# A gated linear-attention chain with two expert layers on one core: domain weights tied to the attention's end, two products moved from GpSimd to VectorE, chunk 1 written ahead of the later gates, zero matmuls between the first chunks

## The chip, the cores and the metric

The program runs on one core of a Trainium2 chip. The metric is the time of the whole program on the device in microseconds (us), lower is better, as the median of several executions.

## The reference, cut to what matters

Three layers follow each other. The first is a recurrent attention over 2 batches, 8 heads, 768 tokens and heads of 40 numbers:

```python
for t in range(S):
    m_new = np.maximum(f_gate[:, :, t] + m, i_gate[:, :, t])
    f_stab = np.exp(f_gate[:, :, t] + m - m_new)
    i_stab = np.exp(i_gate[:, :, t] - m_new)
    C = f_stab * C + i_stab * np.einsum('bhd,bhe->bhde', vt, kt)
    n = f_stab * n + i_stab * kt
    y[:, :, t] = sigmoid(o_gate[:, :, t]) * (C @ qt) / np.maximum(np.abs(n @ qt), 1.0)
```

Its 1536 x 320 result x goes through a layer of 8 experts, of which a noisy gate picks the best two for each token: `out[token] += weight * (relu(x @ w1[e]) @ w2[e])`, with w1[e] of 320 x 1024. What comes out goes through a second layer of 4 experts, all of which see every token, each weighted by a domain weight `p = domain_probs / (sum + 1e-9)`:

```python
for e in range(4):
    out += p[:, e:e + 1] * (np.maximum(x @ w1[e], 0.0) @ w2[e])
```

## The kernel before, in words

The attention works on chunks of 128 tokens: chunks 0 to 5 are batch 0, chunks 6 to 11 batch 1. Within a chunk the recurrence is a masked product; between chunks a state C of 104 x 164 numbers is carried. One chunk consists of small steps, each a function `o_...`: D0 and D1 (L340) build the decay matrix A of four heads each (a matmul `dp`, an exponential on ScalarE, a triangular mask on GpSimd), G (L353) the decay of the carried state (matmul `gp`, exponential `gb`), S (L363) the products of queries and keys (16 matmuls `sp`), M0 and M1 (L373) multiply A by S on VectorE, qg (L378) scales the queries by gb, kw (L384) weights the keys, U (L399) makes the state's update `up`, Cg (L394) decays the state and Cu (L410) adds the update, inter (L420) and AV (L433) accumulate into `hp` what comes from the state and from the chunk, tp (L443) turns the result, x (L449) divides and applies the output gate, xp (L465) turns x again and lg (L475) makes the gate's logits. A number in brackets stands for the chunk in this text: AV(1) is AV of chunk 1.

The gates come in four parts (PARTS, L31): chunk 0, chunk 1, chunks 2 and 3, chunks 4 and 5, with all 12 chunks' rows of both batches in the partitions. `gates` (L255) makes the running maximum and the sums on VectorE, `gates_terms` (L269) turns them into the operands tk and tq of D and G (for the later parts mostly on ScalarE), and `gates_turn` (L292) makes w_t, the key weights, by a transposition and an exponential. The output gate's sigmoid (L299) needs another function table of ScalarE than the exponentials, so a table load stands before and after it; it runs over a whole batch at once, in place in `xs`, into which `og_load` brings the output gates.

The order around the first chunks is written out by hand (L889 to L946). After that the table STEP (L47) says which steps of which chunks stand together: "inter+0" in row 1 of step i is inter(i), "S+1" is S(i+1). PLAN1 and PLAN2 mix these rows (A) with the routing (r, q, f) and the splitting of the first expert weights (w). `done` keeps a step that was already written from being written twice. Beneath this order a scheduler places each engine's instructions by what it estimates to be ready, with the written order as priority; `tc.issue_after(x)` puts what stands inside it behind x. All loads are issued by SyncE's queue in its order. Buffers limit how early a load can go: three each of qt and kv, two of kp.

PSUM has 8 buffers, handed out in turn. Before the first real matmul 24 matmuls of zeros (L889, WARM) run on TensorE. Once the attention of batch 0 is routed, `moe1` runs the first expert layer, with the attention of batch 1 woven in, and `moe2` the second. The domain weights `prob` (L985 to L990) are written after the attention's end in the program's text, with nothing that ties them to it.

Of the kernel before, what the change touches and what calls it, by code (L numbers as in the profile page):

```python
# [45 lines left out]

STEP = [  # L47
    "U+0 D0+2 D1+2 kw+1 M1+0 loadk+2 lg-2 store-2",
    "tp-1 x-1 qg+1 M0+0 inter+0 load+3 Cg+0",
    "G+2",  # L50
    "xp-1 S+1 AV+0 Cu+0",
]


# [11 lines left out]
def body(ctx: ExitStack, tc: tile.TileContext, d, o, dbg=None):  # L66
# [172 lines left out]
    def fi_load(n):  # L239
        nc.sync.dma_start(fi[:, :, n], d["fi"].rearrange("r k (c l) -> r k c l", c=NC)[:, :, n])  # L240
# [51 lines left out]
    def gates_turn(part):  # L292
        n = PARTS[part]
        pt = psum([P, n.stop - n.start, 4, 32], "pt")
        for c in range(n.start, n.stop):
            nc.tensor.transpose(pt[:, c - n.start].rearrange("t q r -> t (q r)"), awr[:, c, :], ident)
            nc.scalar.activation(w_t[:, c].rearrange("t (q p) -> t q p", q=4), pt[:, c - n.start, :, 0:4], AF.Exp)

    def sigmoid(b, after):  # L299
        with tc.issue_after(after):  # L300
            s1 = nc.scalar.preload_act_table_set("sigmoid_and_others")
        with tc.issue_after(s1.ins):
            s2 = nc.scalar.activation(xs[b], xs[b], AF.Sigmoid)
        with tc.issue_after(s2.ins):
            return nc.scalar.preload_act_table_set("natural_log_exp_and_others").ins

    at2_cm = tc.tile_pool(name="at2", bufs=2, side="right")
    at2 = at2_cm.__enter__()
# [31 lines left out]
    def o_decay(i, g):  # L340
        b, c = divmod(i, NC)
        t = st[i]
        if g == 0:
            t["A"] = at2.tile([P, H, P], F32, name="A", bufs=3)
        hs_ = slice(4 * g, 4 * g + 4)
        A = t["A"][:, hs_]
        dp = psum([P, 4, P], "dp")
        r = slice(32 * (2 * b + g), 32 * (2 * b + g) + 32)
        nc.tensor.matmul(dp, tk[r, c], tq[r, c], start=True, stop=True)
        front["act"] = nc.scalar.activation(A, dp, AF.Exp).ins  # L350
        nc.gpsimd.affine_select(A, A, pattern=[[0, 4], [1, P]], compare_op=ALU.is_ge, fill=0.0, base=0, channel_multiplier=-1)

    def o_gb(i):  # L353

        b, c = divmod(i, NC)
        if c > 0:
            gp = psum([104, 4, P], "gp")
            nc.tensor.matmul(gp, over[b], tq[:, c], start=True, stop=True)
            gb = at2.tile([104, 4, P], F32, name="gb", bufs=3)
            nc.scalar.activation(gb, gp, AF.Exp)  # L360
            st[i]["gb"] = gb

    def o_S(i):  # L363
# [9 lines left out]
    def o_M(i, g):  # L373
        t = st[i]
        hs_ = slice(4 * g, 4 * g + 4)
        t["m", g] = front["dve"] = nc.vector.tensor_mul(t["A"][:, hs_], t["sp", g], t["A"][:, hs_]).ins

    def o_qg(i):  # L378
        if i % NC > 0:
            qg = at2.tile([104, 4, P], F32, name="qg")  # L380
            nc.gpsimd.tensor_mul(qg, st[i]["qt"], st[i]["gb"])
            st[i]["qg"] = qg

    def o_kw(i):  # L384
# [5 lines left out]

    def state(k):
        return Cs[k][:, : 4 * 41].rearrange("r (p e) -> r p e", p=4)

    def o_Cg(i):  # L394
        c = i % NC
        if 0 < c < NC - 1:
            nc.gpsimd.tensor_mul(state(1 - c % 2), state(c % 2), st[i]["gb"][:, :, P - 1 : P].to_broadcast([104, 4, 41]))

    def o_U(i):  # L399
        if i % NC < NC - 1:  # L400
# [9 lines left out]
    def o_Cu(i):  # L410
        c = i % NC
        if c < NC - 1:
            up = st[i]["up"]
            cs = state(1 - c % 2)
            if c == 0:
                nc.vector.tensor_copy(cs, up)
            else:
                nc.vector.tensor_add(cs, up, cs)

    def o_inter(i):  # L420
        c = i % NC
# [59 lines left out]
            nc.tensor.matmul(lp, xts[i % 2][:, k, :], wgn[:, k, : 2 * E1], start=(k == 0), stop=(k == 2))  # L481
        nc.scalar.copy(lgs[b][:, c, :], lp)

    OPS = dict(loadk=o_loadk, load=o_load, D0=lambda i: o_decay(i, 0), D1=lambda i: o_decay(i, 1), G=o_gb, S=o_S, M0=lambda i: o_M(i, 0), M1=lambda i: o_M(i, 1), qg=o_qg, kw=o_kw, Cg=o_Cg, U=o_U, Cu=o_Cu, inter=o_inter, AV=o_AV, tp=o_tp, x=o_x, store=o_store, xp=o_xp, lg=o_lg)
    done = set()

    def do(op, i, *a):
        if 0 <= i < NT and (op, i) not in done:
            done.add((op, i))
            OPS[op](i, *a)  # L490

# [394 lines left out]
    def og_load(b):  # L886
        nc.sync.dma_start(xs[b], d["og"][b])

    if WARM:  # L889
        wps = psum([P, 4 * P], "warm")  # L890
        for i in range(WARM):
            nc.tensor.matmul(wps, zero[:, :P], zero, start=(i == 0), stop=(i == WARM - 1))
    do("loadk", 0)
    o_load(0, ("qt",))
    fi_load(slice(2, NC))
    o_load(0, ("kv",))
    og_load(0)
    do("loadk", 1)
    o_load(1)
    nc.sync.dma_start(wgn, d["wgn"])  # L900
    exps = nc.scalar.preload_act_table_set("natural_log_exp_and_others").ins
    with tc.issue_after(last_const):
        last = gates(0)
    with tc.issue_after(last), tc.issue_after(exps):
# [2 lines left out]
    do("S", 0)  # L907
    for op in ("D0", "D1"):
        do(op, 0)
    with tc.issue_after(last):  # L910
        over = [at.tile([P, 104], F32R, name=f"over_{b}") for b in range(B)]
        for b in range(B):
            wide = pro.tile([P, 104], F32, name=f"wide_{b}")
            nc.gpsimd.memset(wide, 0.0)
            for j in range(2):
                nc.vector.tensor_mul(wide[:, 64 * j : 64 * j + D], sums.to_broadcast([P, D]), quarter[:, 2 * b + j : 2 * b + j + 1].to_broadcast([P, D]))
            nc.vector.tensor_copy(over[b], wide)
        last = gates(1)
    with tc.issue_after(last):
        last = gates_terms(1)  # L920
# [1 line left out]
        do(op, 0)  # L922
    gates_turn(1)
    do("U", 0)
    do("inter", 0)
    do("AV", 0)
    do("Cu", 0)
    for op in ("D0", "D1", "G", "S"):
        do(op, 1)
    exps = sigmoid(0, front["act"])  # L930
    done.update((("load", 0), ("load", 1)))
# [3 lines left out]
        last = gates(2)  # L935
    with tc.issue_after(last), tc.issue_after(exps):
        last = gates_terms(2)
    gates_turn(2)
    nc.sync.dma_start(noise, d["noise"])
    og_load(1)  # L940
# [41 lines left out]
        weave(moe1(n), RST, 1, 1)  # L982
    drain(RST)
    drain(A)
    nc.sync.dma_start(prob, d["prob"])  # L985
    nc.vector.tensor_reduce(psm, prob, AX.X, ALU.add)
    nc.vector.tensor_scalar(psm, psm, 1e-9, None, ALU.add)
    nc.vector.reciprocal(psm, psm)
    nc.vector.tensor_mul(prob, prob, psm.unsqueeze(2).to_broadcast([P, NT, E2]))
    nc.sync.dma_start(Pall.rearrange("t p e -> p t e"), prob)  # L990
    if dbg == "x":
        for b in range(B):
            nc.sync.dma_start(o["x"][b].rearrange("p c d -> p c d"), xs[b])
# [93 lines left out]
```

## Time and profile before

| what | us |
|---|---|
| median of 3 runs | 720.25 (720.1 to 725.9) |
| the profiled execution, whole | 719.56 |
| its span, first to last instruction | 717.8 |
| TensorE busy in the span | 690.1 (96%) |
| VectorE busy | 367.1 (51%) |
| ScalarE busy | 258.1 (36%) |
| GpSimd busy | 95.3 (13%) |

The profiled execution is one of the same kernel; 1.8 us of it lie outside the span. Times in the trace count from the span's first instruction. TensorE's clock has two levels: 1.2 and 2.4 GHz. The profile gives the granted share of the higher one, so 0.50 is 1.2 GHz and 1.00 is 2.4 GHz. PE is TensorE, DVE VectorE, ACT ScalarE, POOL GpSimd and SP SyncE; SPq is the queue that issues loads.

### The profile page before, as it was taken

To read this page: it belongs to the slowest core of one execution; us is meant where nothing else is said; L and a number is where in the kernel's file an instruction comes from. 1 tells how busy PE (TensorE), PEld (TensorE's weight loads), DVE (VectorE), ACT (ScalarE), POOL (GpSimd) and SP (SyncE) were. 2 spreads that over 40 slices of the span, in tenths; PEclk is the share of its full clock that TensorE was granted. 3 is DMA by queue.
4 is the path that set the end of the run, shared out by engine and by line. 5 is a ranking of instruction groups with operands and counts; after the bars stand their busy time and mean duration, and the time that the engine had idled before them with its cause. 6 is when DMAs were issued, how large, how long until landed. Compare 5 with 4: busy or idle time off the path is not lost.

```text
span 717.8 us, 11459 instructions
## 1 busy us (share of the span) xinstructions
PE 690.1 (96%) x4528; PEld 625.2 (87%) x4528; DVE 367.1 (51%) x806; ACT 258.1 (36%) x477; POOL 95.3 (13%) x155
## 2 busy tenths in 40 slices
PE   7698879999999999999999999999999999999997
PEld 3476658998999999999989898898998988989987
DVE  7635885798466656657865515413244123332131
ACT  3847532555245434444552304212133022221120
POOL 3423334100522011015105000000000000000000
PEclk8569856999999999999999999999999999999999
DMA  8326554546565444458654003200031001001011
GB/s 268 86 88 205 162 166 134 152 136 221 171 193 154 144 143 138 135 155 253 215 179 129 0 1 86 77 1 0 13 104 47 1 0 36 3 1 37 1 37 40
DMA packets 36434, 73.79 MB, mean 103 GB/s; under 512 B 7576, under 2 KB 14744, under 8 KB 36376
## 3 DMA queue, kind: packets, MB, share of 16 engines
q1 hardware_dynamic: 33752, 64.16, 29.0%
q0 software_dynamic: 2624, 8.85, 4.3%
q8 instruction: 38, 0.62, 0.4%
q14 instruction: 20, 0.16, 0.1%
HBM read 64.07 MB, written 8.92 MB: 102 GB/s over the span
## 4 chain that ended last, share of the span: by engine, by line
PE 82%; DMA 7%; DVE 6%; issue 1%; ACT 1%; SPq 1%; ACTq 0%; DVEq 0%
PE z L207 24%; PE z L221 24%; PE s L207 12%; PE s L221 10%; DMA raw<-w 3%; DMA kv<-kv 2%; PE hp L438 2%; PE hp L431 2%; PE sp L370 2%; PE s L217 1%; DVE w1lo L188 1%; PE lp L481 1%; DMA raw<-v 1%; DMA prob<-prob 1%; PE pa L651 1%
## 5 line engine op out<-in xcount | busy, mean ns | idle before, releaser
L224 ACT ACTIVATE hh<-z 128x512 fp32r<-128x512 f32 x96 | 57.1, 599 | 192.4 <-PE z L207 192.2
L221 PE MATMUL z<-w2hi,hh 128*128 128x320 f32 x384 | 118.6, 309 | 0.0
L221 PE MATMUL z<-w2hi,hl 128*128 128x320 f32 x384 | 118.3, 308 | 0.0
L221 PE MATMUL z<-w2lo,hh 128*128 128x320 f32 x384 | 118.3, 308 | 0.0
L207 PE MATMUL z<-x2h,w1hi 128*128 128x512 f32 x288 | 112.4, 390 | 0.0
L221 PE MATMUL s<-w2hi,hh 128*128 128x320 f32 x448 | 107.4, 312 | 1.3 <-DVE hh L225 0.8
L225 DVE SCALAR_TENSOR_TENSOR hl<-z,hh 128x512 fp32r<-128x512 f32 x96 | 65.8, 690 | 82.5 <-ACT hh L224 82.5
L207 PE MATMUL z<-x2h,w1lo 128*128 128x512 f32 x288 | 96.6, 389 | 0.0
L207 PE MATMUL s<-xh,w1hi 128*128 128x256 f32 (+1 forms) x288 | 85.4, 313 | 0.0
L188 DVE TENSOR_TENSOR w2lo<-raw,w2hi 128x640 fp32r<-128x640 f32 x60 | 49.2, 821 | 65.0 <-ACT w2hi L187 64.9
L221 PEld LDWEIGHTS s<-w2hi,hh 128*128 128x128 f32 x448 | 76.7, 188 | 2.4 <-DVE hh L225 1.3
L207 PE MATMUL z<-x2l,w1hi 128*128 128x512 f32 x192 | 74.8, 390 | 0.0
L188 DVE TENSOR_TENSOR w1lo<-raw,w1hi 128x768 fp32r<-128x768 f32 x60 | 58.1, 969 | 31.5 <-ACT w1hi L187 31.3
L187 ACT CAST w2hi<-raw 128x640 fp32r<-128x640 f32 x60 | 43.5, 728 | 84.2 <-PE s L217 25.1
L221 PEld LDWEIGHTS z<-w2lo,hh 128*128 128x128 f32 x384 | 72.1, 188 | 0.6
L221 PEld LDWEIGHTS z<-w2hi,hh 128*128 128x128 f32 x384 | 72.1, 188 | 0.5
L221 PEld LDWEIGHTS z<-w2hi,hl 128*128 128x128 f32 x384 | 72.1, 188 | 0.0
L207 PE MATMUL s<-xh,w1lo 128*128 128x256 f32 (+1 forms) x288 | 70.6, 309 | 0.0
L221 PE MATMUL s<-w2lo,hh 128*128 128x320 f32 x224 | 69.2, 309 | 0.0
L187 ACT CAST w1hi<-raw 128x768 fp32r<-128x768 f32 x60 | 50.2, 836 | 50.2 <-PE s L207 29.2
L207 PEld LDWEIGHTS z<-x2h,w1lo 128*128 128x128 f32 x288 | 54.1, 188 | 11.3
L207 PEld LDWEIGHTS z<-x2h,w1hi 128*128 128x128 f32 x288 | 54.1, 188 | 10.8
(206 smaller groups left out, 1004.4 us busy)
## 6 DMA issues: line engine op xcount, KB each, us to landing
raw<-w SPq DMA_DIRECT2D x44, 384.0 KB
raw<-w SPq DMA_DIRECT2D x44, 320.0 KB
raw<-v SPq DMA_DIRECT2D x16, 384.0 KB
raw<-v SPq DMA_DIRECT2D x16, 320.0 KB
kv<-kv SPq DMA_DIRECT2D x12, 324.0 KB
Yd<-ys SPq DMA_DIRECT2D x8, 320.0 KB
kp<-kT SPq DMA_DIRECT2D x12, 208.0 KB
qt<-qT SPq DMA_DIRECT2D x12, 208.0 KB
```

The lines of the kernel that those rows point to most:

```text
L187: nc.scalar.copy(hi, raw)
L188: nc.vector.tensor_sub(lo, raw, hi.bitcast(F32))
L207: nc.tensor.matmul(out_ps, l, r, start=(i == 0), stop=(i == len(seq) - 1))
L217: nc.tensor.matmul(yp, both[f], r[:, k], start=(f == 0 and i == 0), stop=(f == NF - 1 and i == 1))
L221: nc.tensor.matmul(yp, l, r, start=(f == 0 and i == 0), stop=(f == NF - 1 and i == 2))
L224: nc.scalar.activation(hh, src, AF.Relu)
L225: nc.vector.scalar_tensor_tensor(hl, src, 0.0, hh.bitcast(F32), ALU.max, ALU.subtract)
L370: nc.tensor.matmul(sp[g][:, j, :], t["kp"][r, j, :], t["qt"][r, j, :], start=True, stop=True)
L431: nc.tensor.matmul(hp[64 * j : 64 * j + m, p, :], Cs[c % 2][r, 41 * p : 41 * p + m], t["qg"][r, p, :], start=(p == 0), stop=False)
L438: nc.tensor.matmul(hp[64 * j : 64 * j + 41, p, :], t["kv"][:, 4 * j + p, D:], t["A"][:, 4 * j + p, :], start=False, stop=(p == 3))
L481: nc.tensor.matmul(lp, xts[i % 2][:, k, :], wgn[:, k, : 2 * E1], start=(k == 0), stop=(k == 2))
L651: nc.tensor.transpose(pk[k][:, c], xe[:r, s, k * P : (k + 1) * P], ident[:r, :r])
```

## The change

1. The domain weights' load and their four VectorE operations stand inside `behind()`, so behind the last load, exponential and mask product that the attention issued.
2. qg goes from GpSimd to VectorE (10 products of 104 x 512). Cg, the decay of the state on GpSimd, goes; Cu does both in one operation per head pair, so four operations of 104 x 41 on VectorE in place of one addition of 104 x 164.
3. The gate operands `over` are made on GpSimd and not on VectorE.
4. D, G and S of chunk 1 are written ahead of inter(0) and AV(0), and kw, M, qg, U, Cu, inter and AV of chunk 1 ahead of the third part of the gates. In STEP Cg goes, and xp stands at the end of its row.
5. The first table load ahead of each sigmoid is no longer written out, and each exponential of D and G is tied behind the load that brings the exponentials' table back.
6. Matmuls of zeros (`fill`) stand at four further places: 8, 6, 4 and 12.
7. The load order: kv(0) ahead of the later gates, and chunk 1's loads ahead of the output gates.

```diff
-            s1 = nc.scalar.preload_act_table_set("sigmoid_and_others")
-        with tc.issue_after(s1.ins):
             s2 = nc.scalar.activation(xs[b], xs[b], AF.Sigmoid)
         with tc.issue_after(s2.ins):
-            return nc.scalar.preload_act_table_set("natural_log_exp_and_others").ins
+            front["table"] = nc.scalar.preload_act_table_set("natural_log_exp_and_others").ins
+        return front["table"]
...
-        front["act"] = nc.scalar.activation(A, dp, AF.Exp).ins
+        with tc.issue_after(front["table"]):
+            front["act"] = nc.scalar.activation(A, dp, AF.Exp).ins
...
-            nc.gpsimd.tensor_mul(qg, st[i]["qt"], st[i]["gb"])
+            nc.vector.tensor_mul(qg, st[i]["qt"], st[i]["gb"])
...
-    def o_Cg(i):
-        c = i % NC
-        if 0 < c < NC - 1:
-            nc.gpsimd.tensor_mul(state(1 - c % 2), state(c % 2), st[i]["gb"][:, :, P - 1 : P].to_broadcast([104, 4, 41]))
...
-                nc.vector.tensor_add(cs, up, cs)
+                for p in range(4):
+                    nc.vector.scalar_tensor_tensor(cs[:, p], state(c % 2)[:, p], st[i]["gb"][:, p, P - 1 : P], up[:, p], ALU.mult, ALU.add)
...
+    def fill(n):
+
         wps = psum([P, 4 * P], "warm")
-        for i in range(WARM):
-            nc.tensor.matmul(wps, zero[:, :P], zero, start=(i == 0), stop=(i == WARM - 1))
+        for i in range(n):
+            nc.tensor.matmul(wps, zero[:, :P], zero, start=(i == 0), stop=(i == n - 1))
...
     do("loadk", 0)
     o_load(0, ("qt",))
+    o_load(0, ("kv",))
     fi_load(slice(2, NC))
-    o_load(0, ("kv",))
-    og_load(0)
     do("loadk", 1)
     o_load(1)
+    og_load(0)
...
+    fill(8)
...
     do("U", 0)
+    do("Cu", 0)
+    fill(6)
+    for op in ("D0", "D1", "G", "S"):
+        do(op, 1)
+    fill(4)
     do("inter", 0)
     do("AV", 0)
-    do("Cu", 0)
-    for op in ("D0", "D1", "G", "S"):
+    for op in ("kw", "M0", "M1", "qg", "U", "Cu"):
         do(op, 1)
     exps = sigmoid(0, front["act"])
...
         last = gates_terms(2)
+    do("inter", 1)
+    do("AV", 1)
+    fill(12)
     gates_turn(2)
...
-    nc.sync.dma_start(prob, d["prob"])
...
+    with behind():
+        nc.sync.dma_start(prob, d["prob"])
...
```

What this does to the engines' orders is seen at three places. The first is TensorE around AV(0): before, hp_315 is chunk 0's accumulator (L426 opens it, L438 is AV), dp_329 and dp_333 are D of chunk 1, gp_337 is G(1) and sp_341 and sp_342 are S(1).

```order
L426 LDWEIGHTS zero
L426 MATMUL hp_315<-zero 105x512
L438 MATMUL hp_315<-A,kv 41x128 x8
L349 MATMUL dp_329<-tq,tk 128x512
L349 MATMUL dp_333<-tq,tk 128x512
L358 MATMUL gp_337<-tq,over_270 104x512
L370 MATMUL sp_341<-qt,kp 128x128
```

The same place with the change, where dp_333 and dp_337 are D of chunk 1, gp_341 is G(1), sp_345 and sp_346 are S(1), warm_325 is the last of six matmuls of zeros; AV(0) follows behind S(1) and four more matmuls of zeros:

```order
L890 LDWEIGHTS zero
L890 MATMUL warm_325<-zero 128x512
L348 MATMUL dp_333<-tq,tk 128x512
L348 MATMUL dp_337<-tq,tk 128x512
L358 MATMUL gp_341<-tq,over_279 104x512
L371 MATMUL sp_345<-qt,kp 128x128
L371 MATMUL sp_346<-qt,kp 128x128
```

D, G and S of chunk 1 moved from behind AV(0) to ahead of it.

The second place is TensorE around inter(1): before, it is hp_478 (L431) and stands behind D of chunk 3 (dp_423), the turn of the last gates (pt_453, L296) and tp(0) (tp_462).

```order
L349 MATMUL dp_419<-tq,tk 128x512
L349 MATMUL dp_423<-tq,tk 128x512
L296 MATMUL pt_453<-ident,awr 128x128
L446 MATMUL tp_462<-ident,hs 128x105 x4
L431 MATMUL hp_478<-qg,C_186 64x128
L431 MATMUL hp_478<-qg,C_186 41x128
```

With the change it is hp_420; AV(1) (L435) stands right behind it, then 12 matmuls of zeros, and only then the turn of the third part of the gates, D of chunks 2 and 3 and tp(0):

```order
L428 MATMUL hp_420<-qg,C_186 64x128
L428 MATMUL hp_420<-qg,C_186 41x128
L435 MATMUL hp_420<-A,kv 41x128 x8
L890 LDWEIGHTS zero
L890 MATMUL warm_439<-zero 128x512
```

inter(1) and AV(1) moved from behind tp(0) to ahead of everything that the third part of the gates feeds.

The third place is VectorE behind the sums of the third part of the gates (L263), before and with the change in one piece. psm and prob are the domain weights, A<-sp are M0 and M1 of chunk 1, asr and awr the rest of the gates.

```order
 L263 SCALAR_TENSOR_TENSOR LF<-reset,lf 128x256
-L986 TENSOR_REDUCE psm<-prob 128x12
+L382 TENSOR_TENSOR qg<-qt,gb 104x512
+L377 TENSOR_TENSOR A<-sp_345,A 128x512
+L377 TENSOR_TENSOR A<-sp_346,A 128x512
 L265 TENSOR_TENSOR asr<-fi,LF 128x256
-L987 TENSOR_SCALAR psm<-psm 128x12
 L266 TENSOR_TENSOR awr<-asr,LF 128x256
-L988 RECIPROCAL psm<-psm 128x12
-L376 TENSOR_TENSOR A<-sp_341,A 128x512
-L376 TENSOR_TENSOR A<-sp_342,A 128x512
-L989 TENSOR_TENSOR prob<-prob,psm 128x48
```

The domain weights left this place; qg(1) came in, and chunk 1's M stands ahead of asr and awr.

## Rows read from the trace of the kernel before

**Rows 1.** Stretches of the span; us, busy per engine (instructions), granted PE clock, DMA share, GB/s

```profile
0.00:11.00 11.00, 8.34 (x43) 3.90 (x43) 7.43 (x31) 2.06 (x4) 5.65 (x57) 1.00 0.77 258
11.00:48.00 37.00, 29.39 (x189) 20.41 (x191) 20.70 (x51) 24.55 (x59) 12.19 (x17) 0.50 0.43 120
48.00:79.50 31.50, 26.98 (x339) 20.73 (x333) 20.22 (x60) 20.45 (x40) 11.18 (x14) 0.99 0.61 186
79.50:86.00 6.50, 6.50 (x49) 5.33 (x47) 4.35 (x17) 3.64 (x9) 1.22 (x2) 0.50 0.37 136
86.00:93.00 7.00, 4.85 (x62) 3.71 (x63) 6.46 (x17) 3.26 (x8) 3.57 (x4) 0.99 0.50 163
93.00:120.30 27.30, 24.00 (x183) 19.54 (x180) 20.13 (x75) 8.50 (x19) 11.46 (x12) 0.50 0.53 157
120.30:717.80 597.50, 590.05 (x3678) 551.55 (x3674) 287.83 (x558) 195.66 (x340) 50.04 (x51) 1.00 0.30 91
```

**Rows 2.** Timeline of PE, 0 to 60 us; start, us, engine, line, what, [idle before, releaser]

```profile
1.39 6.71 PE L892 MATMUL warm<-zero 128*128 128x512 bf16 x24 [1.39 <-POOL zero L84]
...
11.68 0.47 PE L296 MATMUL pt<-ident,awr 128*128 128x128 f32 x1 [1.94 <-DVE awr L266]
...
31.09 0.91 PE L446 MATMUL tp<-ident,hs 105*128 105x105 f32 x4
31.93 1.96 PE L431 MATMUL hp<-qg,C 40*64 40x128 f32 x16
...
43.48 0.94 PE L446 MATMUL tp<-ident,hs 105*128 105x105 f32 x4
```

**Rows 3.** Timeline of ACT, 0 to 60 us

```profile
18.00 1.09 ACT L350 ACTIVATE A<-dp 128x512 f32<-128x512 f32 x2
...
20.89 1.80 ACT L303 ACTIVATE x<-x 128x1920 f32<-128x1920 f32 x1
22.71 1.28 ACT L305 ACT_TABLE_LOAD   x1
24.00 0.41 ACT L272 CAST LFh<-LF 128x256 fp32r<-128x256 f32 x1
...
24.62 0.60 ACT L277 ACTIVATE LF<-LF,mix,kind 128x256 f32<-128x256 f32 x1
...
25.77 2.44 ACT L289 ACTIVATE tq<-LF,head 128x128 fp32r<-128x128 f32 x8
```

**Rows 4.** Timeline of DVE, 0 to 45 us

```profile
13.21 0.33 DVE L416 COPY C<-up 104x164 f32<-104x164 f32 x1 [1.59 <-PE up L407]
...
22.84 0.20 DVE L986 TENSOR_REDUCE psm<-prob 128x12 f32<-128x48 f32 x1 [4.81 <-DMA prob<-prob]
...
25.25 0.48 DVE L278 SCALAR_TENSOR_TENSOR LF<-LFh,mix,LF 128x256 f32<-128x256 f32 x1
...
26.22 0.49 DVE L388 TENSOR_TENSOR kw<-kv,w_t 128x320 f32<-128x320 f32 x1
```

**Rows 5.** SP's queue, 0 to 60 us

```profile
12.45 0.33 SPq L887 DMA_DIRECT2D x<-og  x1
```

**Rows 6.** Timeline of ACT again, around the second sigmoid

```profile
54.10 1.28 ACT L360 ACT_TABLE_LOAD   x1 [0.19 <-PE gp L358]
...
59.42 0.57 ACT L440 COPY hs<-hp 105x512 f32<-105x512 f32 x1
```

**Rows 7.** Timeline of DVE, 57 to 126 us

```profile
69.06 1.56 DVE L388 TENSOR_TENSOR kw<-kv,w_t 128x320 f32<-128x320 f32 x1
```

**Rows 8.** Timeline of POOL, 0 to 130 us

```profile
68.92 1.35 POOL L381 TENSOR_TENSOR qg<-qt,gb 104x512 f32<-104x512 f32 x1 [1.40 <-issue]
```

**Rows 9.** Groups of POOL by form, 12 to 125 us; count, busy, mean ns, idle before

```profile
L381 POOL TENSOR_TENSOR qg<-qt,gb 104x512 f32<-104x512 f32 x10 | 13.7, 1368 | 14.4 <-issue 10.8 <-ACT gb L360 3.4 <-POOL A L351 0.2
```

**Rows 10.** Groups of DVE by form, 12 to 125 us

```profile
L376 DVE TENSOR_TENSOR A<-sp,A 128x512 f32<-128x512 f32 x22 | 14.3, 680 | 15.3 <-PE sp L370 15.3
...
L418 DVE TENSOR_TENSOR C<-up,C 104x164 f32<-104x164 f32 x8 | 2.6, 321 | 2.1 <-PE up L407 2.1
```

More of the change, by code (lines that the diff above doesn't have):

```diff
@@ L48 @@
     "U+0 D0+2 D1+2 kw+1 M1+0 loadk+2 lg-2 store-2",
-    "tp-1 x-1 qg+1 M0+0 inter+0 load+3 Cg+0",
+    "tp-1 x-1 qg+1 M0+0 inter+0 load+3",
     "G+2",
-    "xp-1 S+1 AV+0 Cu+0",
+    "S+1 AV+0 Cu+0 xp-1",
 ]
@@ L359, in o_gb @@
             gb = at2.tile([104, 4, P], F32, name="gb", bufs=3)
-            nc.scalar.activation(gb, gp, AF.Exp)
+            with tc.issue_after(front["table"]):
+                front["act"] = nc.scalar.activation(gb, gp, AF.Exp).ins
             st[i]["gb"] = gb
@@ L482, in o_lg @@
         nc.scalar.copy(lgs[b][:, c, :], lp)
-    OPS = dict(loadk=o_loadk, load=o_load, D0=lambda i: o_decay(i, 0), D1=lambda i: o_decay(i, 1), G=o_gb, S=o_S, M0=lambda i: o_M(i, 0), M1=lambda i: o_M(i, 1), qg=o_qg, kw=o_kw, Cg=o_Cg, U=o_U, Cu=o_Cu, inter=o_inter, AV=o_AV, tp=o_tp, x=o_x, store=o_store, xp=o_xp, lg=o_lg)
+    OPS = dict(loadk=o_loadk, load=o_load, D0=lambda i: o_decay(i, 0), D1=lambda i: o_decay(i, 1), G=o_gb, S=o_S, M0=lambda i: o_M(i, 0), M1=lambda i: o_M(i, 1), qg=o_qg, kw=o_kw, U=o_U, Cu=o_Cu, inter=o_inter, AV=o_AV, tp=o_tp, x=o_x, store=o_store, xp=o_xp, lg=o_lg)
     done = set()
@@ L887, in og_load @@
         nc.sync.dma_start(xs[b], d["og"][b])
-    if WARM:
+    def fill(n):
         wps = psum([P, 4 * P], "warm")
-        for i in range(WARM):
-            nc.tensor.matmul(wps, zero[:, :P], zero, start=(i == 0), stop=(i == WARM - 1))
+        for i in range(n):
+            nc.tensor.matmul(wps, zero[:, :P], zero, start=(i == 0), stop=(i == n - 1))
+    fill(WARM)
     do("loadk", 0)
     o_load(0, ("qt",))
+    o_load(0, ("kv",))
     fi_load(slice(2, NC))
-    o_load(0, ("kv",))
-    og_load(0)
     do("loadk", 1)
     o_load(1)
+    og_load(0)
     nc.sync.dma_start(wgn, d["wgn"])
-    exps = nc.scalar.preload_act_table_set("natural_log_exp_and_others").ins
+    exps = front["table"] = nc.scalar.preload_act_table_set("natural_log_exp_and_others").ins
     with tc.issue_after(last_const):
@@ L909, in body @@
         do(op, 0)
-    with tc.issue_after(last):
[L911 to L917, printed above, removed]
+    fill(8)
+    over = [at.tile([P, 104], F32R, name=f"over_{b}") for b in range(B)]
+    for b in range(B):
+        wide = pro.tile([P, 104], F32, name=f"wide_{b}")
+        nc.gpsimd.memset(wide, 0.0)
+        for j in range(2):
+            nc.gpsimd.tensor_mul(wide[:, 64 * j : 64 * j + D], sums.to_broadcast([P, D]), quarter[:, 2 * b + j : 2 * b + j + 1].to_broadcast([P, D]))
+        nc.gpsimd.tensor_copy(over[b], wide)
+    with tc.issue_after(last):
         last = gates(1)
@@ L984, in body @@
     drain(A)
-    nc.sync.dma_start(prob, d["prob"])
[L986 to L990, printed above, removed]
+    with behind():
+        nc.sync.dma_start(prob, d["prob"])
+        nc.vector.tensor_reduce(psm, prob, AX.X, ALU.add)
+        nc.vector.tensor_scalar(psm, psm, 1e-9, None, ALU.add)
+        nc.vector.reciprocal(psm, psm)
+        nc.vector.tensor_mul(prob, prob, psm.unsqueeze(2).to_broadcast([P, NT, E2]))
+        nc.sync.dma_start(Pall.rearrange("t p e -> p t e"), prob)
     if dbg == "x":
```

## The prediction

> **What bounds the kernel now.** I read the stretches of the span first, because the share of busy time on the page mixes stages with different limits. From 120.3 us on TensorE is busy for 590.05 of 597.50 us at the full clock [rows 1]: this is the two expert layers, whose work the change leaves alone. So the time is the start of that dense part plus 597.5, and the question is how much sooner than 120.3 us it starts. Before it, TensorE has the half clock from 11 to 48 us, from 79.5 to 86 and from 93 to 120.3, and is busy there for 29.39 of 37, 6.50 of 6.50 and 24.00 of 27.30 us [rows 1]. ScalarE is busy for 24.55 of the first 37 us.
>
> Then I read the timelines of the first 60 us. TensorE waits 1.94 us for the gates of chunk 1 [rows 2]; from about then the clock is halved. ScalarE starts the exponentials of chunk 1 at 18.00, the sigmoid at 20.89, the table load behind it at 22.71, and only at 24.00 the third part of the gates, whose tq (25.77, lasting 2.44) feeds D of chunks 2 and 3 [rows 3]. tp(0) starts on TensorE at 31.09, inter(1) at 31.93, tp(1) at 43.48 [rows 2]. The largest single wait is VectorE's: 4.81 us for the domain weights [rows 4], which only the last layer uses.
>
> **The change part by part.** Durations and starts are those of the profiled execution; minus is sooner.
>
> *Domain weights behind the attention.* The wait of 4.81 us goes [rows 4]. By itself I cost this at nothing: what VectorE has to do next for the gates (25.25, L278) needs ScalarE's LF, which starts at 24.62 and takes 0.60, so ends at 25.22 [rows 3, 4]. ScalarE would have been late without VectorE's wait. It must go, though, for the next term to count. Bounds: 0 to -1.
>
> *Chunk 1 ahead of the rest.* D(1) stood behind AV(0) on TensorE and now stands ahead of it. What is last for it then is tq(1), for which VectorE's operation stood behind the copy of the state at 13.21, itself waiting 1.59 us for U(0) [rows 4]; in the new order the copy stands behind it. I take the exponentials of chunk 1 from 18.00 to 15.0, -3.0; the bounds are -1.5 (tq no sooner, only AV(0) out of the way) and -3.5. ScalarE now copies AV(0)'s result between sigmoid and table load, 0.57 as in rows 6, so the third part of the gates starts at 24.00 - 3.0 + 0.57 = 21.57, -2.4. Does the sigmoid's load arrive in time, 740 KB further back in the queue? The second og load went out at 12.45, having waited for the first one's completion, so the first had landed by then [rows 5]. At the 258 GB/s of the first 11 us [rows 1], 740 KB (chunk 1's q, k and v) take 2.9 us: 15.4, and it is wanted at about 17. Hidden.
>
> From 24.00 to tp(0) at 31.09 there are 7.09 us of gates and D of chunks 2 and 3; the same steps from 21.57 give 28.7, -2.4.
>
> *inter(1) and AV(1) ahead of tp(0).* From tp(0) to tp(1) there are 12.4 us, at the half clock. Of this inter(1) took 1.96 [rows 2], and AV(1), as many matmuls with as many columns, I price the same; both go into TensorE's idle time before 28 us (7.6 of the 37 us are idle, [rows 1]). So tp(1) comes after 12.4 - 3.9 = 8.5 us, at 37.2 and not at 43.48: -6.3. Bounds: -3.5 (if qg(1) or M(1) come too late on VectorE and AV(1) holds up ScalarE's copy ahead of tq) and -7.5.
>
> *Table loads.* In the second sigmoid's place an exponential (L360) came between the two loads and fetched its own table, 1.28 us, after which the sigmoid's was loaded again; the copy of AV(3)'s result waited behind them until 59.42, and tp(3) behind it [rows 6]. Two loads go, 2.56 us of ScalarE. The sigmoid still stands ahead of that copy, and TensorE needs some 2 us from G(4) to AV(3)'s end anyway (S and AV, at the full clock half of 1.96 each), so I count half: -1.3; bounds 0 and -2.6. The Trainium skill ("ScalarE: Activation LUTs", What ACT_TABLE_LOAD costs) puts a switch at about 2.66 us, the load and a drain of 1.38 behind it. Here the next operation starts 1.29 us after a load's start (22.71 to 24.00, [rows 3]), so no drain is seen; by the page this edit would be worth up to 5.3 us.
>
> *qg and the state's decay on VectorE.* Not shown on VectorE before. On GpSimd a qg took 1.37 [rows 9]; on VectorE the nearest row is M (0.68, same length, [rows 10]), so ten are 6.8 us. Four operations of 104 x 41 come for one of 0.32 [rows 10]: at least 0 more (the same elements), at most 4 x 0.32 - 0.32 = 1.0 each; I take 0.5, eight times, 4 us. Against it stands what VectorE lost to GpSimd: kw took 1.56 us while GpSimd ran qg from 68.92, and 0.49 at 26.22 when it did not, so 1.07 for one qg [rows 4, 7, 8]. Ten would be 10.7 if each met such an operation, 0 if none. From 66 to 108 us, where VectorE is closest to its limit, four qg and three Cu come in (2.7 + 1.5) and about as much goes. I take 0; bounds -4 and +4.2. The Trainium skill ("SBUF — State Buffer", two separate sides) says that VectorE and GpSimd share one pair of ports, held for a whole instruction by whoever starts first, also by a VectorE operation with two SBUF inputs. The kw row agrees. It speaks against the change as well: a qg on VectorE, with two SBUF inputs, would hold off GpSimd's masks, up to 0.68 each.
>
> *Zero matmuls.* 24 took 6.71 us [rows 2], 0.28 each, so 8, 6, 4 and 12 of them take 2.2, 1.7, 1.1 and 3.4 us at the full clock, twice that at half. The first fill the wait of 1.94, the last the time up to D(2) at 25 us. Cost 0; at the half clock the last 12 end about 1.5 us late, so bounds 0 and +1.5. What they may bring is the clock: it was halved when TensorE had stood idle, and they stand in its gaps up to about 24 us. Bounds: 0 if the clock halves all the same, and -5 if it stays full until 48 us. In that case tp(0) to tp(1) shrinks from 8.5 to about 6 (then tq(4) on ScalarE is last), and the 4.8 us from 43.5 to 48.3 to half. Behind the last fill tp(0), G, S, xp and U follow with waits between them, so I expect the clock to fall there and to come back sooner than at 48: a third, -1.7.
>
> *GpSimd's `over`*: six short operations there instead of on VectorE, done well before G(1): 0.
>
> Sum: -6.3 - 1.3 + 0 + 0 - 1.7 = -9.3. The profiled execution took 719.6, its span 717.8, so 710.3 for such an execution; the median of the runs (720.25) lies 0.7 higher: 711.
>
> **The rivals.**
>
> *A. The clock holds.* For it: matmuls of full length stand in every gap from 9 to 24 us. Against: behind them TensorE has little to do until tp(0). The full -5 in place of -1.7 makes -12.6: 707.6, and down to 703.6 if the stretch from 93 to 120.3 [rows 1] also gains a third of its 12 us.
>
> *B. VectorE sets the pace later.* In 66 to 108 us it is nearly full; if GpSimd's masks hold it up as its qg did, the +4.2 stands, and with late fills +1.5: -9.3 + 5.7 = -3.6, 716.6. For it: the change adds some 11 us to VectorE. Against: the kw row.
>
> *C. The early load order misfires.* If og lands after 17 us, sigmoid, gates and all behind them wait one for one; with 3 us, -6.3: 714.
>
> *D. Slower: the clock is lost in the stretches that had it.* From 48 to 79.5 and 86 to 93 TensorE did 31.83 us of work at the full clock, with 6.67 us idle [rows 1]. The change thins out the work behind 28 us and alters every gap; at the half clock all the way this work would take 31.8 us more, of which the idle time absorbs 6.7: +25, less 7.6 gained: 737.7. It ends slower than before as soon as a third of these stretches is lost. Nothing in the rows speaks for it except that the clock did fall at 79.5 and at 93.
>
> *E. It doesn't do what it says:* no wait but the 4.81 goes, which was hidden; 720.
>
> **How the numbers follow.** The sum as worked out, 707 to 714: 0.46. A 0.19, B 0.20, C 0.05, D 0.05, E 0.05. The range 703.5 to 717 takes in A and B and C. A change of 1% (7.2 us) is about what a measurement of this kernel can tell, so faster means under 713.0: the sum's case mostly (0.42), A (0.19), a little of C and B (0.05): 0.66. Within 1%: 0.29. Slower: D, 0.05.
>
> **What would show it.** Right: no wait for prob on VectorE; ScalarE's third part of the gates at about 21.5 us; tp(0) near 28.7 and tp(1) near 37; no table load in front of an exponential that follows the sigmoid's table; the first expert matmul near 111 us; 597.5 us from there. Wrong: a granted clock of 0.50 in 48 to 79.5 us, kw and M on VectorE still above 1 us, ScalarE waiting for og, or a dense part that is longer than before.

## The result, and the profile after

The changed kernel takes 711.51 us (median of 11 runs, 708.7 to 716.9) beside 724.12 us for the kernel before (11 runs, 718.5 to 731.8): a ratio of 0.983 by these medians, and of 0.985 as reported, with a 95% interval of 0.981 to 0.989. The forecast was 711.0 in a range of 703.5 to 717.0. The number was right, and so was the sign; the change is 12.6 us between these medians and 8.0 us between the spans of the two profiled executions, where -9.3 was forecast from a median of 720.25. As the experiments show, the number came out right by luck: what gained is not what the forecast added up. In the groups of experiments below, the reported intervals leave out runs more than 1.5% above a kernel's own fastest, which takes away most runs of the kernel before in the second and third groups and has the changed kernel itself at 0.995 there, so that I compare kernels by their medians over all runs.

The stretches of the changed kernel's profiled execution (span 709.8, whole 711.51) answer to [rows 1]. Columns: stretch and length, then busy time and (instructions) of PE, PEld, DVE, ACT, POOL, the granted PE clock, DMA share, GB/s.

```profile
0.00:29.30 29.30, 26.03 (x195) 14.50 (x199) 22.89 (x60) 20.16 (x45) 12.63 (x71) 0.99 0.70 221
29.30:56.10 26.80, 25.27 (x189) 19.16 (x186) 12.92 (x38) 13.29 (x32) 2.64 (x5) 0.50 0.28 83
56.10:77.30 21.20, 20.07 (x248) 15.74 (x248) 17.39 (x61) 12.18 (x30) 5.34 (x8) 0.98 0.75 243
77.30:107.10 29.80, 28.67 (x227) 22.18 (x223) 23.93 (x104) 12.67 (x26) 7.18 (x8) 0.50 0.44 130
107.10:110.20 3.10, 3.10 (x43) 2.75 (x39) 2.20 (x7) 1.17 (x4) 0.94 (x1) 1.00 0.45 92
110.20:709.80 599.60, 591.28 (x3674) 553.19 (x3672) 291.85 (x568) 195.72 (x341) 51.41 (x51) 1.00 0.31 93
```

The experts start at 110.2 and no longer at 120.3 us, 10.1 sooner. The dense part lasts 599.6 and not 597.5 (one wait of 2.04 us of TensorE at 168 us, with a short fall of the clock behind it, lies in it), so 8.0 us of span are left. The clock is the surprise of this table: it is full up to 29.3 us, where before it was half from 11 us on, and then half for 26.8 us in which TensorE has work for 25.27. Before, those steps had the full clock from 48 us.

ScalarE's timeline answers to [rows 3] and, from 50 us, to [rows 6]. Columns: start, duration, engine, line, operation.

```profile
14.81 1.08 ACT L350 ACTIVATE A<-dp 128x512 f32<-128x512 f32 x2 [0.52 <-PE dp L348]
...
16.40 1.28 ACT L301 ACT_TABLE_LOAD   x1
17.69 1.80 ACT L301 ACTIVATE x<-x 128x1920 f32<-128x1920 f32 x1
...
19.99 1.28 ACT L303 ACT_TABLE_LOAD   x1
21.28 0.40 ACT L272 CAST LFh<-LF 128x256 fp32r<-128x256 f32 x1
...
52.55 1.80 ACT L301 ACTIVATE x<-x 128x1920 f32<-128x1920 f32 x1
54.52 0.58 ACT L437 COPY hs<-hp 105x512 f32<-105x512 f32 x1 [0.17 <-PE hp L435]
...
55.95 1.28 ACT L303 ACT_TABLE_LOAD   x1
57.24 1.09 ACT L350 ACTIVATE A<-dp 128x512 f32<-128x512 f32 x2
```

Chunk 1's exponentials start at 14.81 (15.0 was expected), the sigmoid finds its gates loaded at 17.69, and the third part of the gates starts at 21.28 (21.57 expected). At the second sigmoid no exponential fetches a table of its own any more.

TensorE's timeline answers to [rows 2]. The tp lines are tp(0), the end of tp(1), tp(2) and the end of tp(3); xp is the first turning of an output, with the longest wait of this stretch ahead of it.

```profile
27.61 0.53 PE L443 MATMUL tp<-ident,hs 105*128 105x105 f32 x4
...
32.09 0.69 PE L466 MATMUL xp<-ident,x 128*128 128x128 f32 x2 [1.53 <-DVE x L456]
...
36.06 0.77 PE L443 MATMUL tp<-ident,hs 105*128 105x105 f32 x3
...
47.08 0.94 PE L443 MATMUL tp<-ident,hs 105*128 105x105 f32 x4
...
57.29 0.47 PE L443 MATMUL tp<-ident,hs 105*128 105x105 f32 x3
```

tp(1) comes 7.4 us sooner than before (43.48), tp(3) only 2.8 (57.29 for 60.04), the start of the experts 10.1. So 4.6 us of the front's gain were given back between 36 and 57 us, and 7.3 came in from elsewhere later. That is what the experiments had to explain.

### The profile page after: what moved, and what is told of

Read it like the earlier page. It is cut to its first block, busy times and chain, and to the rows that moved or that the text cites. A ratio compares the mean times of both kernels' runs of the same rounds, so it can differ in the third digit from the quotient of the medians.

```text
span 709.8 us, 11516 instructions
## 1 busy us (share of the span) xinstructions
PE 694.4 (98%) x4556; PEld 627.5 (88%) x4558; DVE 371.2 (52%) x834; ACT 255.2 (36%) x475; POOL 80.1 (11%) x143
## 4 chain that ended last, share of the span: by engine, by line
PE 86%; DVE 6%; DMA 3%; ACT 2%; issue 1%; POOL 1%; ACTq 0%; DVEq 0%; POOLq 0%
PE z L207 25%; PE z L221 24%; PE s L207 14%; PE s L221 11%; PE sp L371 2%; DMA raw<-w 2%; PE hp L428 1%; PE hp L435 1%; PE s L217 1%; PE lp L478 1%; DMA raw<-v 1%; DVE w1lo L188 1%; PE pa L648 1%; PE up L403 1%; PE xp L466 1%
```

## The experiments

Twelve kernels ran in three groups of four, each group on one chip beside the kernel before. Kernels of different groups are compared by their ratios to it, which is good to a few us. "To before" is the ratio of the medians, and the reported ratio with its interval stands beside it. "Half" is the median over a kernel's runs of the time at half clock, worked out as 2 x (1 - mean granted clock) x span. In group 1 one of the 23 runs of the kernel before took 1325.36 us; the median of the times holds it, the one of half clock does not.

```
group  kernel                                    us      to before  reported (95%)           half, us
  1    before                                    727.65  1          -                         86
  1    before, qg and decay on VectorE           709.33  0.975      0.979 (0.974 to 0.984)    49
  1    before, domain weights tied               725.54  0.997      0.995 (0.990 to 1.000)    83
  1    changed, qg and decay on GpSimd           721.16  0.991      0.992 (0.989 to 0.996)    62
  1    changed, no fills                         715.30  0.983      0.984 (0.978 to 0.990)    72
  2    before                                    725.68  1          -                         87
  2    changed                                   710.79  0.979      0.995 (0.989 to 1.001)    58
  2    changed, idle work on GpSimd              712.61  0.982      0.995 (0.990 to 1.001)    52
  2    changed, waits filled                     706.64  0.974      0.983 (0.975 to 0.991)    32
  2    before, VectorE move and weights tied     710.78  0.979      0.989 (0.982 to 0.995)    60
  3    before                                    726.15  1          -                         87
  3    before, waits filled                      718.76  0.990      0.999 (0.994 to 1.005)    57
  3    changed, qg alone on GpSimd               712.88  0.982      0.992 (0.986 to 0.998)    56
  3    before, both parts, waits filled          706.65  0.973      0.986 (0.980 to 0.991)    37
  3    changed, more waits filled                700.68  0.965      0.976 (0.970 to 0.982)    11
```

**1. The move to VectorE alone.** In the kernel before:

```diff
-            nc.gpsimd.tensor_mul(qg, st[i]["qt"], st[i]["gb"])
+            nc.vector.tensor_mul(qg, st[i]["qt"], st[i]["gb"])
-    def o_Cg(i):
...
-                nc.vector.tensor_add(cs, up, cs)
+                for p in range(4):
+                    nc.vector.scalar_tensor_tensor(cs[:, p], state(c % 2)[:, p], st[i]["gb"][:, p, P - 1 : P], up[:, p], ALU.mult, ALU.add)
```

> The kernel before with one part of the change alone: the scaled queries and the state's decay move from GpSimd to VectorE. Theory (what slows the steps of before is that GpSimd's multiplications stretch VectorE's own: kw 1.56 us where it is 0.49 alone): from chunk 2 on the steps get shorter, kw and the scaled queries take 0.5 to 0.7 us each, and the time falls by 3 to 5 us. Rival (VectorE gets 1.1 us a chunk more and is the engine that the end of the steps waits for): up to 4 us slower. Rival (the prediction's value): within 1 us of the kernel before. The dense part keeps its 597 us in all three.

Measured: 18.3 us under before, at least as much as the whole change gives. None of the three expectations allowed for so much. Its runs spent 49 us at half clock and not 86; at the 0.37 us for each of them that experiment 5 gives, an estimated 13.7 of the 18.3 us are the clock. The stretches of its execution show where the half clock lay:

```profile
11.90:38.90 27.00, 18.23 (x117) 11.83 (x118) 17.41 (x45) 20.30 (x48) 5.39 (x8) 0.50 0.47 118
38.90:80.00 41.10, 36.66 (x471) 28.61 (x471) 31.38 (x110) 28.14 (x61) 7.38 (x12) 1.00 0.66 200
80.00:92.80 12.80, 12.80 (x103) 9.99 (x101) 8.70 (x36) 3.90 (x10) 1.22 (x2) 0.50 0.26 82
92.80:96.60 3.80, 2.09 (x25) 1.67 (x22) 3.80 (x16) 1.74 (x4) 1.32 (x2) 0.89 0.71 220
96.60:102.20 5.60, 5.24 (x40) 4.24 (x40) 3.97 (x24) 1.42 (x3) 2.13 (x2) 0.54 0.19 63
```

The first stretch at half clock lies in the front, where TensorE has work for only 18.23 of 27.00 us, and the steps from 38.9 to 80 run at full clock. A step at full clock takes 6.2 us (tp(2) at 48.28, tp(3) at 54.48), at half clock about 11.5 (tp(7) at 86.89, tp(8) at 98.34 in the changed kernel). So it also matters what lies under the half clock, and not only how long it lasts.

**2. The move taken back in the changed kernel**, with the same lines reversed.

> The changed kernel with the scaled queries and the decay put back on GpSimd, all else as changed. Theory (contention with GpSimd costs the steps their time): slower than the changed kernel by 3 to 5 us, with kw at 1.0 to 1.6 us again and the gap between the transposes of chunks 4 and 6 back above 14 us (it was 14.81 before, 11.61 after). Rival (the gain of 8 us after the change comes from the early chunk 1 and the clock alone): within 1 us of the changed kernel.

Measured: 721.16, a ratio of 0.991 to before, where the changed kernel has 0.979 (group 2) to 0.983 (the first comparison): the move is worth some 6 to 8 us on top of the rest, and the rest alone 6.5. Alone the two are worth 18.3 and 6.5, together 14.9: they don't add up. From tp(4) to tp(6) it takes 20.6 us, more than the 14 expected, but kw takes 0.48 us from 55 us on and not 1.0 to 1.6. One x was stretched there (1.58 us at 76.57, beside a qg on GpSimd), but it held TensorE up nowhere: the clock was half for 34.70 us, and TensorE was never idle in them:

```profile
45.00:54.40 9.40, 8.38 (x109) 6.49 (x108) 3.30 (x10) 7.19 (x13) 3.16 (x4) 1.00 0.53 161
54.40:89.10 34.70, 34.70 (x256) 26.48 (x255) 19.36 (x67) 13.25 (x32) 8.46 (x11) 0.51 0.45 142
```

**3. Without the fills.** `fill(8)`, `fill(6)`, `fill(4)` and `fill(12)` taken out; the 24 at the start stay.

> The changed kernel without the four groups of zero matmuls; those at the very start stay. Theory (they hold the granted clock until 29.3 us): TensorE is at half clock from about 11 us, as before, the exponentials of chunk 1 and the transposes of chunks 0 and 1 come 2 to 4 us later, but the clock comes back before 56 us, so that the first expert matmul moves by 0 to +3 us. Rival 1 (the zero matmuls only take TensorE's time, 8 matmuls of 0.43 us at half clock being 3.4 us at the last group): 1 to 4 us faster than the changed kernel. Rival 2 (without them the clock is half up to 56 us all the same): 4 to 7 us slower than the changed kernel.

Measured: 0.983 of before. That is 0 to 2.5 us above the changed kernel, inside what a comparison across groups can tell. TensorE spent 72 us at half clock and not 58. In the profile the clock fell at 12.6 us, so most of the 14 us lay in the front, where TensorE waits anyway. Rival 1 falls, and so does the price of rival 2, though the clock came back only at 57 us, as that rival had it. The theory's 0 to +3 stands; its 2 to 4 us for the early transposes don't (tp(0) at 29.07 for 27.61).

**4. Domain weights alone.** In the kernel before, the six lines on `prob` and `psm` go into `with behind():`.

> The kernel before with one part of the change alone: the domain weights' load and the VectorE work on them are tied to the end of the attention. Theory of the prediction (the 4.81 us for which VectorE waits there lie beside ScalarE's table loads, sigmoid and third gates, whose end is no more than 0.03 us ahead of VectorE's own): the wait is gone from VectorE, the transpose of chunk 0 still comes at 30.5 to 31.1 us, and the time stays within 1 us of the kernel before. Rival (VectorE's wait is on the path): the transposes of chunks 0 and 1 come 4 to 5 us sooner, and the time falls by 4 to 5 us.

Measured: 2.1 us under before (0.990 to 1.000), tp(0) at 30.46 for 31.09 and tp(1) at 42.84 for 43.48. The trace shuts the rival out: the transposes come 0.6 us sooner and not 4 to 5. The times alone would not, since their interval reaches from 0 to 7 us, and they don't tell 0 from 2.

**5. The changed kernel again**, unchanged, in the second group.

> The changed kernel once more, beside the others of this group. Both theories: its ratio to the kernel before lies in the interval that it had (0.981 to 0.989). Theory (how long TensorE runs at half clock ahead of the experts differs from execution to execution): where a stretch of half clock begins and ends moves by some us against the first profile (29.3 to 56.1 and 77.3 to 107.1). Rival (the program fixes the clock): both stretches stand within 1 us of those.

Measured: 710.79, 0.979 of before by medians (the reported 0.995 is the case spoken of above). Both numbers lie outside the 0.981 to 0.989 that was expected, one on either side. The clock theory holds: in this execution (714.1 us span) half clock lay at 31.3 to 44.4, 54.7 to 71.7, 84.7 to 99.0 and 102.4 to 119.5 us, and not at 29.3 to 56.1 and 77.3 to 107.1. One profile is a sample of the clock, not its course. Over the 35 runs of the kernel before in this group the time goes with the mean granted clock from 711.79 us at 0.965 to 741.15 at 0.916. A line through them gives 0.37 us for each us at half clock, with a correlation of 0.99.

**6. Is it contention?** In the changed kernel, behind qg:

```diff
+            idle = at2.tile([104, 4, P], F32, name="idle")
+            nc.gpsimd.tensor_mul(idle, st[i]["qt"], st[i]["gb"])
```

> The changed kernel plus one multiplication of the size of the scaled queries on GpSimd in each chunk, whose result nobody reads; VectorE does all that it did. Theory (GpSimd's work stretches VectorE's when both run): kw and the scaled queries on VectorE go from 0.5 to 0.7 us to 1.0 to 1.6 us where they lie beside it, and the kernel is 3 to 6 us slower than the changed kernel. Rival (the gain came from the shorter chain from the gates' exponential to the state's matmuls, 0.67 us on VectorE for 1.37 us on GpSimd, and GpSimd's work by itself costs nobody anything): within 1.5 us of the changed kernel.

Measured: 712.61 beside 710.79, 1.8 us more, near the rival's 1.5; but the runs of each scatter over 10 us, so that the times alone don't part 1.8 from the theory's 3. The order of the other engines' instructions is the same as in the changed kernel. VectorE's groups from 26 to 120 us, first of the changed kernel:

```profile
L382 DVE TENSOR_TENSOR qg<-qt,gb 104x512 f32<-104x512 f32 x9 | 6.5, 721 | 3.6 <-ACT gb L361 3.6
...
L389 DVE TENSOR_TENSOR kw<-kv,w_t 128x320 f32<-128x320 f32 x8 | 5.0, 639 | 0.8 <-DMA kv<-kv 0.8
L456 DVE TENSOR_TENSOR x<-xo,rd 128x320 f32<-128x320 f32 x10 | 4.8, 484 | 0.1
```

and of the one with idle work:

```profile
L382 DVE TENSOR_TENSOR qg<-qt,gb 104x512 f32<-104x512 f32 x9 | 6.5, 720 | 3.7 <-ACT gb L361 3.7
L458 DVE TENSOR_TENSOR x<-xo,rd 128x320 f32<-128x320 f32 x10 | 5.9, 590 | 0.1
...
L391 DVE TENSOR_TENSOR kw<-kv,w_t 128x320 f32<-128x320 f32 x8 | 5.7, 718 | 0.0
```

GpSimd's work stretches kw from a mean of 639 to 718 ns and x from 484 to 590, 1.7 us of VectorE in all. Contention is there, but it is far smaller than the move's gain.

**7. Which of the two operations?** In the changed kernel only qg goes back to `nc.gpsimd`; the decay stays fused on VectorE.

> The changed kernel with the scaled queries alone back on GpSimd; the decay stays on VectorE, fused with the update. Theory 1 (the scaled queries are what cost on GpSimd: the state's matmuls wait for them): 6 to 10 us slower than the changed kernel, as with both back (721.2 against 710.8 to 711.5 us). Theory 2 (the decay is what cost: it waits on GpSimd for TensorE to have read the state, and the masks of the next decays queue behind it): within 2 us of the changed kernel.

Measured: 712.88, 0.982 of before: as the changed kernel within a comparison across groups. With both back it was 0.991. So the some 7 us (0.991 less 0.982) come with the decay on GpSimd, or with the two there together; the decay alone on GpSimd was not run. Theory 2 holds as to the operation. Its mechanism (waiting for TensorE's read of the state, masks queued behind) was only argued: neither here nor in the kernel before does a view of the waits name an engine that waited for GpSimd's C (in the kernel of experiment 10 VectorE did once, 2.93 us at 111.67).

The traces show something else that comes with the decay's place: the scheduler gives VectorE another order. With both back on GpSimd, four splittings of expert weights (w2lo) stand ahead of the last half of the first batch's routing (rh), for which TensorE then waits 4.57 us:

```profile
102.81 0.82 DVE L188 TENSOR_TENSOR w2lo<-raw,w2hi 128x640 fp32r<-128x640 f32 x1
...
104.27 0.81 DVE L188 TENSOR_TENSOR w2lo<-raw,w2hi 128x640 fp32r<-128x640 f32 x1
...
105.65 0.81 DVE L188 TENSOR_TENSOR w2lo<-raw,w2hi 128x640 fp32r<-128x640 f32 x1
...
106.56 0.81 DVE L188 TENSOR_TENSOR w2lo<-raw,w2hi 128x640 fp32r<-128x640 f32 x1
...
108.52 0.35 DVE L568 TENSOR_TENSOR rh<-in_col,place 128x64 bf16<-128x64 bf16 x2
108.80 0.40 PE L573 MATMUL pt<-rh,oh 128*128 128x64 bf16 x4 [4.57 <-DVE rh L568]
```

With qg alone on GpSimd they stand behind it, and TensorE waits 0.43 us:

```profile
99.42 0.78 DVE L564 TENSOR_TENSOR rh<-in_col,place 128x64 bf16<-128x64 bf16 x2
99.68 0.27 PE L569 MATMUL pt<-rh,oh 128*128 128x64 bf16 x2 [0.43 <-DVE rh L564]
...
100.91 0.82 DVE L188 TENSOR_TENSOR w2lo<-raw,w2hi 128x640 fp32r<-128x640 f32 x1
```

It is so in all the traces: three or four splittings stand ahead of rh in the four kernels with the decay on GpSimd, none in the nine with the decay on VectorE. With both back on GpSimd, 2.3 us of these splittings lie on the chain of work that ended last; with qg alone, none do. So a part of the some 7 us is this order. What the rest is, and what GpSimd's own time costs, stays open.

**8. The waits of the changed kernel filled.** More zero matmuls where TensorE idled, in the bank that is written next, as here ahead of the output transposes, and likewise ahead of AV(7) and the routing's table:

```diff
+        if i == 0:
+            for _ in range(9):
+                nc.tensor.matmul(xp.rearrange("r p l -> r (p l)"), zero[:, :P], zero[:, : 3 * P], start=True, stop=True)
```

> The changed kernel with more zero matmuls where TensorE idled just ahead of a fall of the clock: 15 for 12 ahead of the gates of chunk 2, 9 ahead of the first transposes of the outputs (a wait of 1.53 us on VectorE), 4 ahead of the values of chunk 7 (a wait of 0.89 us) and 5 ahead of the routing's table (1.13 us). They lie in waits and add at most 1.5 us. Theory (the clock falls behind idle time of TensorE): full clock through 29.3 us and through 77.3 us, 5 to 13 us less for each stretch of 27 to 30 us that is kept, so 5 to 20 us faster than the changed kernel. Rival (the clock falls though TensorE is kept busy): both stretches at half clock stay, and the time is 0 to 1.5 us above the changed kernel.

Measured: 706.64, 4.2 us under the changed kernel beside it, half clock 32 us and not 58 (95% interval of the difference of the medians, by resampling the runs: 1.4 to 9.7 us). The 5 us were missed by a little. VectorE and GpSimd run the same instructions in the same order as in the changed kernel up to 100 us, so here nothing but the zero matmuls is new to them. In the profile the clock still fell, at 36, 54 and 88 us, behind or within waits that were left: 0.95 and 0.84 us at 32 to 35, 0.96 at 51, 4.58 at 87 to 91.

**9. VectorE move and domain weights, the front as before.** Experiments 1 and 4 together.

> The kernel before with two parts of the change: the scaled queries and the decay on VectorE, and the domain weights tied to the attention's end. Theory (the front of before is hidden behind ScalarE's chain and the move to VectorE is what gains): within 2 us of the kernel with the move alone, 2.0% under the kernel before. Rival (with GpSimd out of the way VectorE's wait for the domain weights is on the path): 3 to 5 us faster than with the move alone.

Measured: 710.78 beside 710.79 for the whole change. With the move in place, the early chunk 1, the fills, the table loads and `over` are worth nothing together that these runs can tell.

**10. The waits of the kernel before filled**, nothing else changed in the program: 52 zero matmuls, written as in experiment 8.

> The kernel before with zero matmuls in five of TensorE's waits behind 58 us and nothing else: 8 ahead of the transposes of chunk 3 (a wait of 1.61 us), 3, 15 and 5 ahead of the transposes of the outputs of chunks 3, 5 and 6 (0.46, 2.45 and 0.77 us), 6 and 15 in the second half of the first routing (1.38 and 3.30 us). Theory (a wait of TensorE is followed by a fall of its clock, and of the gain of the whole change more than half is clock): TensorE spends 15 to 30 us less at half clock and the time falls by 5 to 10 us, though no wait is removed. Rival (the waits themselves cost, and the clock falls whatever TensorE does): within 2 us of the kernel before.

Measured: 7.4 us under before by medians, and half clock 57 us in the place of 87, as the theory has it. No work was removed; TensorE does more. By resampling the runs, the medians differ by 3.5 to 12.4 us (95%), while the reported ratio, 0.999, shows no difference; the fastest runs of both are alike (711.63 and 712.03). So the zero matmuls make a good course of the clock frequent and don't beat it. The 30 us at 0.37 each would be 11 us. One thing besides the clock changes: from 79 us on the scheduler orders VectorE's work otherwise too. Its stretches:

```profile
15.00:48.10 33.10, 27.06 (x173) 19.11 (x171) 17.86 (x44) 21.18 (x49) 11.55 (x15) 0.50 0.35 103
48.10:111.50 63.40, 57.54 (x654) 42.03 (x655) 47.19 (x160) 34.33 (x72) 26.03 (x30) 1.00 0.60 186
111.50:116.50 5.00, 5.00 (x39) 4.47 (x39) 3.38 (x10) 1.66 (x4) 2.07 (x3) 0.66 0.40 90
```

From 48 us on the clock stays full for 63.4 us, where before it was lost from 79.5 to 86 and from 93 to 120.3 [rows 1].

**11. The better version: all waits of the changed kernel filled.** Experiment 8 with 15 zero matmuls ahead of the first output transposes, 4 and 5 ahead of logits 0 and 2, 9 and 20 ahead of the routing's table.

> The changed kernel with zero matmuls in all waits that the first such version still showed: 15 in the place of 9 ahead of the first output transposes, 4 and 5 ahead of the first and third logits, 9 and 20 ahead of the two halves of the first routing's table. Theory (each further wait that is filled keeps the clock up): less than 30 us at half clock ahead of the experts, and 3 to 8 us under the first such version (706.6 us there, 710.8 for the changed kernel beside it). Rival (what can be kept is kept, the added matmuls now delay the steps): 0 to 4 us slower than the first such version.

Measured: 700.68 (697.3 to 701.1), 0.965 of before where the changed kernel has 0.979, so 0.985 of the changed kernel, and some 6 us under experiment 8. All its runs lie below every run of the changed kernel. Its stretches:

```profile
0.00:28.50 28.50, 26.00 (x190) 13.98 (x194) 22.00 (x58) 19.29 (x43) 11.81 (x70) 1.00 0.73 227
28.50:32.40 3.90, 3.90 (x25) 2.52 (x26) 3.90 (x11) 2.72 (x9) 1.08 (x2) 0.56 0.26 77
32.40:98.00 65.60, 63.73 (x730) 46.76 (x732) 52.28 (x195) 35.74 (x84) 16.09 (x21) 1.00 0.53 162
98.00:695.70 597.70, 589.90 (x3674) 551.68 (x3672) 293.45 (x573) 197.18 (x342) 52.12 (x51) 1.00 0.31 94
```

The experts start at 98.0 and not at 110.2 us, and half clock is down to 3.9 us of the profile.

**12. The same on the kernel with experiment 9's two parts**, whose four late waits are filled.

> A candidate that is better than both: the kernel before with the scaled queries and the decay on VectorE, the domain weights tied to the attention's end, and zero matmuls in its four late waits (8 and 4 ahead of the output transposes of chunks 5 and 6, 9 and 7 ahead of the two halves of the first routing's table), with nothing moved in the front. Theory (the clock is what is left to gain): 8 to 20 us less at half clock than without the zero matmuls, 3 to 7 us faster than the 710.8 us measured there. Rival: no change of the clock and 0 to 2 us slower.

Measured: 706.65, 0.973 of before where it was 0.979 without, some 4.5 us, and 37 us at half clock for 60, somewhat more than the 8 to 20 us expected. The changed kernel with all its waits filled is 6.0 us faster in the same group (700.68), but it has 11 us at half clock and not 37. So what the early front is worth once the clock is held, apart from the fills in it, these runs don't show.

## Why the prediction was right, and where its steps were not

- *The bound.* Right: what lies ahead of the experts decides. The dense part stayed within 2.1 us of 597.5.
- *Domain weights, 0 (bounds 0 to -1).* Right that the 4.81 us were hidden behind ScalarE: without them tp(0) comes 0.6 us sooner (experiment 4). The time was 2.1 us less, with an interval that reaches from nothing to 7 us.
- *Chunk 1 ahead and inter(1), AV(1), -6.3.* The places came out (15.0, 21.57, 28.7 and 37.2 expected; 14.81, 21.28, 27.61 and 36.06 seen). The step that failed is the one left unsaid: that what is gained at tp(1) is carried to the end. The steps that were moved forward fell under the half clock of 29.3 to 56.1, and 4.6 of 7.4 us were gone by tp(3). Beside the move to VectorE the whole front is worth nothing that the runs can tell (710.79 and 710.78, experiment 9).
- *Table loads, -1.3.* The extra loads went as described; what that was worth was not measured by itself.
- *qg and decay on VectorE, 0 (bounds -4 and +4.2).* This is the term that was mis-sized most: -18.3 alone, -6 to -8 on top of the rest (experiments 1 and 2). It was weighed as VectorE's time against contention, and both are small. What the term left out is the clock, by the estimate of experiment 1 some 13.7 of the 18.3 us, and what comes with the decay on GpSimd, VectorE's order among it (experiment 7). By the Trainium skill ("SBUF — State Buffer", two separate sides) a VectorE operation with two inputs in SBUF and a GpSimd operation that reads SBUF shut each other out of one pair of ports. The stretched kw of experiment 6 agrees in direction (a mean of 639 and 718 ns).
- *Zero matmuls 0, clock -1.7.* The four fills do keep the clock up to 29.3, and cost and bring next to nothing (experiment 3). That the clock would be back before 48 us was wrong; in the profile it came at 56.1, so that one of the signs of being wrong, half clock in 48 to 79.5 us, did show in part. Taken over all runs the clock is, by estimate, the larger part of the gain: 87 us at half clock before and 58 after, at 0.37 us each, are 10.7 of 14.9 us. This overlaps with the term above; the two aren't to be added. Experiment 8 shows that the clock is cause and not company: it adds zero matmuls alone, leaves VectorE's order as it was, and gains 4.2; experiment 10 gains 7.4.
- *So the sum* of -9.3 was near the 8.0 us of the two profiles because a front that was counted in full stood for a move that was counted at nothing. That is luck. Rival A, the clock holding, is what the changed kernel could have had: 707.6 was worked out for it, 700.7 was reached once the later waits were filled as well. B, C and D did not come: VectorE didn't set a slower pace, the gates' load was in time, and the clock lost in one stretch was won in others.

## What to carry to other kernels

Where TensorE waits for a microsecond or two in a stretch of small matmuls, the wait may cost less than the half clock behind it. Before moving work about, fill such waits with zero matmuls in the bank that is written next, and read the time at half clock of every run, not of one profile. Two edits that each gain alone may share the same gain, so measure each without the other; and when an operation of half a microsecond changes its engine, the scheduler may order the other engines' work anew. So move it alone, and compare the engines' orders before laying the difference to the operation.

## What was not expected of the hardware

The clock stays at half while TensorE is fully busy: 34.70 busy of 34.70 us in experiment 2, 28.67 of 29.80 in the changed kernel. Falls came behind waits, but not behind each one, and the length of the wait doesn't tell which. In the changed kernel the clock was half from 29.3 us on, with no wait over 0.66 us between 24 and 29.3; the wait of 1.53 us came after the fall. In the kernel of experiment 1, waits of 0.65 and 1.24 us at 63 and 69 us passed at full clock, and one of 2.11 with one of 0.43 behind it was followed by the fall at 80:

```profile
77.94 0.29 PE L568 MATMUL pt<-rh,oh 128*128 128x64 bf16 x4 [2.11 <-DVE rh L563]
...
79.09 0.41 PE L465 MATMUL xp<-ident,x 128*128 128x128 f32 x2 [0.43 <-DVE nl L511]
79.33 0.27 PE L466 MATMUL xp<-ident,x 128*64 128x128 f32 x1
79.53 1.69 PE L370 MATMUL sp<-qt,kp 40*128 40x128 f32 x16
```

There sp takes 1.69 us, a mix of the 1.16 that it takes at the full clock in the step before and the 2.08 at half. No run here tells when exactly the clock falls. Two executions of the same changed kernel differ by 5.4 us whole (711.51 and 716.86 in the first comparison) with nearly the same mean clock (0.955 and 0.953), so where the half clock lies counts as well as how long it lasts.
